# Linear attention and two expert layers in split half precision: last layer-1 output blocks in large buffers, a fixed tile for the inverse roots, weight maxima through HBM, weight differences and the inverse-root product on VectorE

## The chip, the cores and the metric

The program runs on one core of a Trainium2 chip. The metric is the device time of one execution in microseconds. TensorE does the matrix products, VectorE (DVE in the rows), ScalarE (ACT) and GpSimd (POOL) prepare operands and empty the accumulators, and every transfer is issued by SyncE (SP), one after another in program order.

## The reference, cut to what matters

```python
kv  = einsum('bhsd,bhse->bhde', k, v)            # 8 batches, 8 heads, 576 tokens, 64 wide
out = einsum('bhsd,bhde->bhse', q, kv)
x   = out / sqrt(mean(out*out, -1) + 1e-6) * g_norm   # 4608 x 512
h   = x @ w_in;   x1 = maximum(0.01*h, h) @ w_out       # 512 -> 2048 -> 512
h   = x1 @ w2_in; y  = (h - tanh(h)) @ w2_out           # 512 -> 2048 -> 512
```

The weights come as 64-bit floats and the kernel reads them as pairs of 32-bit words.

## The kernel before, in words

The work runs in five stages: a head (first attention batches, first weight matrix), "up 1" (x times w1, the attention of the other batches woven in), "down 1" (times w2, giving x1), "up 2" (x1 times w3, tanh) and "down 2" (times w4, the output). Every factor is split into a high and a low half-precision part, and a product is three matmuls. Blocks of two by two are multiplied by a scheme with seven products instead of eight; `PROD` says which sum of the left blocks meets which sum of the right blocks, and `Blocks` collects the seven products in the accumulator banks a, b, c and d.

Operands are made in chains. `left_stages` (L426) makes those of an activation tile: ScalarE rounds three blocks to the high part (`opa`), VectorE subtracts for the low part, four sums of blocks follow (two on VectorE, two on GpSimd in "down", all four on GpSimd in "up"), and ScalarE and VectorE make high and low part of the sums (`ops`). `right_stages` (L358) does the same for a 128 x 512 unit of a weight matrix, `wo` being the result; its four differences of 128 x 128 blocks are GpSimd's (`less`, L374). `convert` (L293) turns the 64-bit words of a unit into a 32-bit float, stores it to HBM (`wf`), and after the last unit `weight_scale` (L249) finds the power of two that scales the matrix. Only then does `split_late` (L387) load the units again, split them and store the result (`wd`), which `load_weights` fetches when the layer before has let go of the weight tiles. w2 and w3 are converted and w2 is split in up 1; w3 is split in down 1; w4 is converted and split in up 2.

The order of all this is not written down. `Plan` is an event list with assumed durations: `fit` looks for a free stretch on ScalarE, VectorE or GpSimd ("A", "V", "G"), and each engine then gets its instructions in the order of these planned moments. On the chip each engine works its list in that order, and a waiting instruction holds up all behind it.

Working buffers come from three pools, each handed out first in, first out: 21 large ones ("l", 4,608 bytes a partition), 12 middle ones ("m", for weight units, `wo` and `opa`) and 8 small ones ("x", 1,152 bytes). A buffer counts as free in the plan as soon as its store is issued, so the next writer may wait on the chip until that store has landed. The small pool holds the temporary results that ScalarE copies out of bank a (`Blocks.keep`, the tiles c, u), the x1 blocks on their way to HBM (`xst`), the attention's `qt` and `sq`, and the inverse roots `iv` of a batch.

The attention of a batch ends in `norms` (L903): ScalarE takes roots, VectorE inverts (`iv`), `iv` is stored to HBM, read back as rows broadcast over the partitions (`bc`), and GpSimd multiplies the batch's two activation tiles by it (L934).

## Time and profile before

| | |
|---|---|
| device time, three runs | 1527.73 us median (1526.67 to 1530.34) |
| the profiled execution | 1526.35 us, of which its span is 1524.6 us |
| TensorE | busy 1443.4 us (95% of the span) |
| VectorE, ScalarE, GpSimd | busy 1247.2 us (82%), 911.2 us (60%), 759.8 us (50%) |
| TensorE's granted clock | 0.979 of full speed in the mean |
| share of the chain that ended last | TensorE's line L495 (all products of the layers) 42.7%, VectorE 3%, GpSimd 1%, transfers 1% |

TensorE is the engine whose work fills the span. A microsecond counts here if it is idle time of TensorE, or TensorE's time at the lower of its two clocks.

### The profile page before, as it was taken

The numbers are of one execution on the slowest core, as the hardware profiler recorded it, in microseconds if no ns is written. First come the engines' busy times: TensorE is split into PE (matmuls) and PEld (weight loads), VectorE is DVE, ScalarE is ACT, GpSimd is POOL, SyncE is SP. The second block draws the span as 40 slices with busy tenths as digits, with TensorE's granted clock in tenths as the row PEclk, the third lists the DMA queues.
The fourth block names the chain that finished last, engine by engine and source line by source line (L and its number), as shares of the span: only waits on it lengthen the run. The fifth ranks groups of instructions, "written<-read, shape, count | busy, mean of one in ns | idle before, by whom it ended". The sixth has DMA issues, their size and how long they took to land. (4 is left out here: it accounts for less than half of the span.)

```text
span 1524.6 us, 33192 instructions
## 1 busy us (share of the span) xinstructions
PE 1443.4 (95%) x12658; PEld 1191.6 (78%) x12658; DVE 1247.2 (82%) x1971; ACT 911.2 (60%) x1525; POOL 759.8 (50%) x758
## 2 busy tenths in 40 slices
PE   5299999999999999999999899999999899999998
PEld 3167777777777777777777688888888788888887
DVE  4886786777777889899996788988899988888881
ACT  5377766777777645455443577778888544454540
POOL 0483321443643455666673355558896644444440
PEclk8599999999999999999999999999999999999999
DMA  9718987999968756446546666655669644444431
GB/s 264 201 60 257 282 281 250 283 295 313 323 250 317 288 172 208 160 168 207 184 146 214 228 221 209 210 200 209 246 240 353 226 146 149 144 143 156 145 97 36
DMA packets 191040, 323.19 MB, mean 212 GB/s; under 512 B 55712, under 2 KB 133536, under 8 KB 190880
## 3 DMA queue, kind: packets, MB, share of 16 engines
q1 hardware_dynamic: 190880, 321.07, 63.6%
q8 instruction: 99, 1.62, 0.4%
q14 instruction: 61, 0.50, 0.1%
HBM read 190.84 MB, written 130.15 MB: 211 GB/s over the span
## 5 line engine op out<-in xcount | busy, mean ns | idle before, releaser
L495 PEld LDWEIGHTS <-w 128*128 128x128 f16 x8400 | 818.3, 98 | 212.1 <-issue 38.1
L474 POOL TENSOR_TENSOR gl<-gl 128x256 f32<-128x256 f32 (+1 forms) x272 | 305.9, 1126 | 297.9 <-issue 92.6
L495 PE MATMUL ps_a<-ops,w 128*128 128x288 f16 (+1 forms) x2400 | 330.3, 281 | 6.0 <-ACT u L544 3.1
L495 PE MATMUL ps_c<-ops,w 128*128 128x288 f16 (+1 forms) x2352 | 314.0, 282 | 6.9 <-DVE g L557 6.8
L495 PE MATMUL ps_a<-opa,w 128*128 128x288 f16 (+1 forms) x2016 | 285.2, 282 | 12.5 <-ACT u L548 6.6
L495 PEld LDWEIGHTS <-ops 128*128 128x128 f16 x1728 | 169.7, 98 | 24.7 <-issue 4.2
L495 PE MATMUL ps_b<-opa,w 128*128 128x288 f16 (+1 forms) x1200 | 175.6, 283 | 0.0
L376 POOL TENSOR_TENSOR unit<-unit 128x128 f32<-128x128 f32 x192 | 129.6, 677 | 91.4 <-DVE wo L369 57.1
L474 DVE TENSOR_TENSOR gl<-gl 128x256 f32<-128x256 f32 (+1 forms) x272 | 160.7, 594 | 4.1
L1213 POOL TENSOR_TENSOR g<-g,th 128x512 f32<-128x512 f32 x72 | 116.7, 1623 | 78.2 <-ACT th L1210 76.8
L934 POOL TENSOR_TENSOR xg<-xg,bc 128x1152 f32<-128x1152 f32 x16 | 47.4, 2970 | 186.3 <-DMA bc<-iv 118.1
L435 ACT ACTIVATE ops<-gl 128x1152 f16<-128x1152 f32 x64 | 74.3, 1162 | 108.7 <-POOL gl L474 107.0
L437 ACT ACTIVATE ops<-gl,inv 128x1024 f16<-128x1024 f32 x72 | 82.5, 1146 | 94.4 <-POOL gl L474 94.4
L495 PEld LDWEIGHTS <-opa 128*128 128x128 f16 x1296 | 126.6, 98 | 14.8
L444 DVE SCALAR_TENSOR_TENSOR ops<-gl,inv,ops 128x1024 f16<-128x1024 f32 x72 | 103.4, 1436 | 22.8 <-ACT ops L437 22.8
L442 DVE TENSOR_TENSOR ops<-gl,ops 128x1152 f16<-128x1152 f32 x64 | 96.5, 1509 | 11.1 <-ACT ops L435 11.0
L495 PE MATMUL ps_a<-w,ops 128*128 128x256 f16 x864 | 97.5, 275 | 3.6 <-ACT c L548 3.6
L557 DVE SCALAR_TENSOR_TENSOR g<-ps_c,u 128x288 f32<-128x288 f32 x128 | 58.0, 453 | 52.1 <-PE ps_c L495 45.8
L548 ACT ACTIVATE u<-ps_a,up 128x256 f32<-128x256 f32 x144 | 67.9, 472 | 51.8 <-PE ps_a L495 41.6
L495 PE MATMUL ps_c<-w,ops 128*128 128x256 f16 x864 | 97.3, 273 | 0.2 <-DVE osb L557 0.2
L474 POOL TENSOR_TENSOR x1g<-x1g 128x256 f32<-128x256 f32 x72 | 64.0, 890 | 49.8 <-DVE opa L444 42.0
L369 DVE SCALAR_TENSOR_TENSOR wo<-unit,s_w,wo 128x384 f16<-128x384 f32 (+1 forms) x96 | 85.3, 892 | 3.7 <-ACT wo L366 3.6
(122 smaller groups left out, 2147.6 us busy)
## 6 DMA issues: line engine op xcount, KB each, us to landing
g<-g SPq DMA_DIRECT2D x64, 576.0 KB, 5.6
gl<-g SPq DMA_DIRECT2D x64, 576.0 KB, 4.8
g<-g SPq DMA_DIRECT2D x72, 512.0 KB, 3.4
gl<-g SPq DMA_DIRECT2D x72, 512.0 KB, 4.5
wd<-wo SPq DMA_DIRECT2D x48, 448.0 KB, 4.2
w<-wd SPq DMA_DIRECT2D x24, 896.0 KB, 7.7
words<-in_moe_w_in_dram SPq DMA_DIRECT2D x64, 256.0 KB, 5.6
words<-in_moe_w_out_dram SPq DMA_DIRECT2D x64, 256.0 KB, 4.6
```

What stands on the lines that cost most here:

```text
L369: nc.vector.scalar_tensor_tensor(out=dst()[:, 1, a:b], in0=cols(0, n), scalar=scale(), in1=dst()[:, 0, a:b], op0=ALU.mult, op1=ALU.subtract,)
L376: nc.gpsimd.tensor_tensor(out=o, in0=a, in1=b, op=ALU.subtract)
L435: nc.scalar.activation(out=o, in_=i_, func=AF.Copy)
L437: nc.scalar.activation(out=o, in_=i_, func=AF.Identity, scale=scale())
L442: nc.vector.tensor_tensor(out=o, in0=i_, in1=h, op=ALU.subtract)
L444: nc.vector.scalar_tensor_tensor(out=o, in0=i_, scalar=scale(), in1=h, op0=ALU.mult, op1=ALU.subtract)
L474: lambda: e.tensor_tensor(out=g()[:, o], in0=g()[:, a], in1=g()[:, b], op=op),
L495: nc.tensor.matmul(out=out_, lhsT=a, rhs=c, start=start and m == 0, stop=stop and m == n - 1, skip_group_check=not fresh,)
L548: nc.scalar.activation(out=t, in_=src, func=AF.Identity, scale=self.scale)
L557: nc.vector.scalar_tensor_tensor(out=o, in0=src, scalar=self.minus if sub else self.scale, in1=t, op0=ALU.mult, op1=ALU.add,)
L934: nc.gpsimd.tensor_tensor(out=x, in0=x, in1=held[kk].ap, op=ALU.mult)
L1213: e.tensor_tensor(out=g()[:, n], in0=g()[:, n], in1=held["t"].ap[:, n], op=ALU.subtract)
```

## The change

It has seven parts.

1. `iv` no longer takes a small buffer; it has a tile of its own for all batches.
2. In the last of the eight rounds of down 1 the x1 blocks go to large buffers, four blocks in one, and leave in four stores of 128 x 576 instead of eight of 128 x 288. The small pool keeps the temporaries alone there.
3. For w2, w3 and w4 the maximum over the partitions is no longer taken with a transpose and a small matmul on TensorE. `far_scale` stores the column of 128 maxima to HBM, reads it back broadcast to all partitions, and VectorE takes the maximum of each row. The planner gives this 26 units of its time instead of 8.8, so the splits of w2 and w4 are planned later (w2 from START + 219 instead of 200, w4 24 later).
4. The differences of a weight unit become three instructions: `both` makes two of them at once (128 x 2 x 128), `less` the other two. For this the words are loaded in another block order, two signs change and `PROD` is renumbered. For w2, w3 and w4 all three are VectorE's; for w1 they stay GpSimd's.
5. From batch 2 on, the product of the activation tiles with `bc` is VectorE's, each tile in two halves, planned 10.5 after the load instead of 7.5.
6. The attention of the batches from 5 on is woven in 5 products earlier per batch.
7. If the plan finds a pool empty, the step is tried again 0.4 later (`NoRoom`); before, this was an error. VectorE's sums in `left_stages` are planned shorter.

```diff
-PROD = {1: (6, 6), 2: (4, 4), 3: (0, 5), 4: (5, 0), 5: (3, 2), 6: (1, 1), 7: (2, 3)}
+PROD = {1: (6, 5), 2: (4, 4), 3: (0, 6), 4: (5, 0), 5: (3, 1), 6: (1, 2), 7: (2, 3)}
...
-                def run(fn=fn):
-                    fn()
+                def run(fn=fn, until=None):
+                    try:
+                        fn()
+                    except NoRoom:
+                        assert until is None or self.now < until, "no room"
+                        self.at(self.now + 0.4, lambda: run(fn, until or self.now + 40.0))
+                        return
...
+    def far_scale(name, m, t):
+        held = {}
+        def put():
+            held["d"] = scratch([P, 1], F32, f"m_{name}_d")
+            nc.sync.dma_start(out=held["d"], in_=m)
+        def get():
+            held["w"] = const.tile([P, P], F32, tag="rows", name=f"rows_{name}")
+            nc.sync.dma_start(out=held["w"], in_=held["d"].rearrange("p o -> o p").broadcast_to((P, P)))
+        def end():
+            r, s = stile(f"r_{name}"), stile(f"s_{name}")
+            nc.vector.tensor_reduce(out=r, in_=held["w"], axis=AX.X, op=ALU.max)
+            powers(r, s)
+        at(t, put)
+        at(t + 6.0, get)
+        at(t + 24.0, end)
...
-        at(t + 2.8 + (later and later + 2.0), last)
+        at(t + (2.8 if n == 0 else 26.0), last)
...
-        def less(o, a, b):
+        def both(e):
+            b = w().rearrange("p (o c) -> p o c", c=P)
+            e.tensor_tensor(out=b[:, 1:4:2], in0=b[:, 3:4].broadcast_to((P, 2, P)), in1=b[:, 1:3], op=ALU.subtract)
+
+        def less(o, a, b, e):
             o, a, b = (w()[:, P * n:P * n + P] for n in (o, a, b))
-            nc.gpsimd.tensor_tensor(out=o, in0=a, in1=b, op=ALU.subtract)
+            e.tensor_tensor(out=o, in0=a, in1=b, op=ALU.subtract)
...
+        on, e = ("V", nc.vector) if merged else ("G", nc.gpsimd)
+        f = 0.28 if merged else 0.5
...
-            ("G", 0.5, lambda: less(t1, b12, b11)), ("G", 0.5, lambda: less(t3, b22, b12)),
-            ("G", 0.5, lambda: less(t2, b22, t1)),
-            ("G", 0.5, (lambda: less(t4, b21, t2)) if minus4 else (lambda: less(t4, t2, b21))),
+            (on, 1.5 * f, lambda: both(e)), (on, f, lambda: less(t2, b22, t1, e)),
+            (on, f, (lambda: less(t4, b21, t2, e)) if minus4 else (lambda: less(t4, t2, b21, e))),
...
-                on, (1.4 if on == "V" else 2.4) * f + 0.1,
+                on, 1.1 * f + 0.08 if on == "V" else GPS * f + 0.1,
...
-            held["iv"] = X.take([4 * Q, T1], F32, "iv")
+            held["iv"] = const.tile([4 * Q, T1], F32, tag="iv", name="iv")
...
-            nc.gpsimd.tensor_tensor(out=x, in0=x, in1=held[kk].ap, op=ALU.mult)
-            L.give(held[kk])
+            e.tensor_tensor(out=x, in0=x, in1=held[kk].ap[:, n0:n1], op=ALU.mult)
+            if n1 == 4:
+                L.give(held[kk])
...
+            if b >= 2:
+                scaled_ = [("V", 0.66, lambda kk=kk, n=n: scale(kk, nc.vector, n, n + 2)) for n in (0, 2)]
+            else:
+                scaled_ = [("G", 2.9 if b else 2.7, lambda kk=kk: scale(kk, nc.gpsimd, 0, 4))]
+            more.append([(None, LOADBC if b > 1 else 7.5 if b else 6.0, lambda kk=kk: load(kk))] + scaled_ + stages)
...
-            pos[b, PAIRS[hp]] = FIRST[b][hp] if b in FIRST else NOP * (NP * b - 16 + 2 * hp)
+            pos[b, PAIRS[hp]] = FIRST[b][hp] if b in FIRST else NOP * (NP * b - 16 + 2 * hp) - 5 * (b - 4)
...
-    spread(lambda i, kk, t: split_late(1, i, kk, t, M), UNITS, START + 200.0, end1 - 75.0)
+    spread(lambda i, kk, t: split_late(1, i, kk, t, M), UNITS, START + 219.0, end1 - 72.0)
...
+            if s == NS1 - 1:
+                if (s, m) not in out_t:
+                    out_t[s, m] = L.take([P, 2, 2, T1], F32, "xst"), []
+                return out_t[s, m][0].ap[:, int(blk[1]) - 1, int(blk[0]) - 1]
...
+                there.append((t, nh))
+                if {(0, nh), (1, nh)} <= set(there):
+                    done_.update((("x1", c, s, 0), ("x1", c, s, 1)))
+                    nc.sync.dma_start(out=x1d[c, s], in_=tile_.ap[:, nh].rearrange("p a b -> p (a b)"))
+                if len(there) == 4:
+                    L.give(out_t.pop((s, m))[0])
...
-    e = c3 + 18.0
+    e = c3 + 42.0
```

Where the instructions stand. On GpSimd before, around the products of batch 6 (`xg<-xg,bc`) with the differences of w2's units (`unit`) and the sums of the attention tile:

```order
L376 TENSOR_TENSOR unit<-unit 128x128 x20
L934 TENSOR_TENSOR xg<-xg,bc 128x1152 x2
L376 TENSOR_TENSOR unit<-unit 128x128 x2
L474 TENSOR_TENSOR xg<-xg 128x288
L376 TENSOR_TENSOR unit<-unit 128x128
```

On VectorE now, at the products of the same batch; `g<-ps` are the adds that empty an accumulator bank:

```order
L602 SCALAR_TENSOR_TENSOR g<-ps_c,u_5006 128x288
L979 TENSOR_TENSOR xg<-xg,bc 128x576
L908 COPY xg<-po 128x288
L379 SCALAR_TENSOR_TENSOR unit<-words,unit 128x512
L419 TENSOR_TENSOR unit<-unit 128x128
L415 TENSOR_TENSOR unit<-unit 128x2x128
L602 SCALAR_TENSOR_TENSOR g<-ps_c,u_5160 128x288
L979 TENSOR_TENSOR xg<-xg,bc 128x576
L419 TENSOR_TENSOR unit<-unit 128x128
L602 SCALAR_TENSOR_TENSOR g<-ps_b,c_5150 128x288
L360 TENSOR_SCALAR unit,mw<-unit 128x512
L979 TENSOR_TENSOR xg<-xg,bc 128x576
```

Four half products and the differences of the weight units have moved from GpSimd's list into VectorE's, and the adds that empty banks c and b stand behind them.

On VectorE before, at the end of up 2, where the first operand of down 2 is made (`opa<-gl`) and w4's last parts are split (`wo<-unit`):

```order
L557 SCALAR_TENSOR_TENSOR g<-ps_c,up_11272,u_15331 128x256
L444 SCALAR_TENSOR_TENSOR opa<-gl,inv_10683,opa 128x768
L369 SCALAR_TENSOR_TENSOR wo<-unit,s_w_13522,wo 128x512
L557 SCALAR_TENSOR_TENSOR g<-ps_b,up_11272,c_15434 128x256
L474 TENSOR_TENSOR gl<-gl 128x256
L1213 TENSOR_TENSOR g<-g,th 128x512
L557 SCALAR_TENSOR_TENSOR g<-ps_c,up_11272,u_15517 128x256
```

The same place now:

```order
L488 SCALAR_TENSOR_TENSOR opa<-gl,inv_10641,opa 128x768
L419 TENSOR_TENSOR unit<-unit 128x128
L602 SCALAR_TENSOR_TENSOR g<-ps_c,up_11221,u_15429 128x256
L518 TENSOR_TENSOR gl<-gl 128x256
L602 SCALAR_TENSOR_TENSOR g<-ps_c,up_11221,u_15313 128x256
L1276 TENSOR_TENSOR g<-g,th 128x512
L518 TENSOR_TENSOR gl<-gl 128x256
L408 SCALAR_TENSOR_TENSOR wo<-unit,s_w_13719,wo 128x512
L602 SCALAR_TENSOR_TENSOR g<-ps_b,up_11221,c_15419 128x256
L488 SCALAR_TENSOR_TENSOR opa<-gl,inv_10641,opa 128x768
```

A difference and two parts of the split (one more follows eight rows below the first) now stand behind the first operand of down 2, where one part stood.

On SyncE the stores of the last x1 blocks and the loads of w3 before and, in the second piece, now:

```order
L421 DMA w_5_11026<-wd_5_306 128x3584
L1103 DMA x_2_7_100<-xst 128x288
L1103 DMA x_3_7_108<-xst 128x288
L1103 DMA x_2_7_100<-xst 128x288
L1103 DMA x_0_7_84<-xst 128x288
L1103 DMA x_3_7_108<-xst 128x288
L421 DMA w_6_11088<-wd_6_307 128x3584
L1103 DMA x_1_7_92<-xst 128x288
L421 DMA w_7_11154<-wd_7_308 128x3584
```

```order
L465 DMA w_5_10976<-wd_5_306 128x3584
L1165 DMA x_2_7_100<-xst 128x576
L1165 DMA x_0_7_84<-xst 128x576
L1165 DMA x_3_7_108<-xst 128x576
L465 DMA w_6_11036<-wd_6_307 128x3584
L1165 DMA x_1_7_92<-xst 128x576
L465 DMA w_7_11102<-wd_7_308 128x3584
```

Fewer stores stand between the loads of the last weight tiles; each waits for two blocks.

## Rows read from the trace of the kernel before

**Rows 1.** TensorE's timeline, six places; brackets: idle before, and what ended it

```profile
265.34 0.90 PE L495 MATMUL ps_a<-opa,w 128*128 128x288 f16 x6 [1.23 <-ACT u L546]
...
377.51 0.86 PE L495 MATMUL ps_a<-opa,w 128*128 128x288 f16 x5 [2.14 <-ACT u L546]
...
754.25 0.77 PE L495 MATMUL ps_a<-opa,w 128*128 128x288 f16 x5 [1.13 <-DVE opa L442]
...
852.07 1.23 PE L495 MATMUL ps_a<-opa,w 128*128 128x256 f16 x5 [6.64 <-ACT u L548]
...
1183.73 0.82 PE L495 MATMUL ps_c<-ops,w 128*128 128x256 f16 x6 [1.75 <-DVE g L557]
...
1203.82 2.50 PE L495 MATMUL ps_a<-w,ops 128*128 128x256 f16 x12 [3.56 <-ACT c L548]
```

**Rows 2.** ScalarE's timeline at two of these places

```profile
376.75 0.41 ACT L853 ACTIVATE sq<-po 128x288 f32<-128x288 f32 x1 [4.36 <-DMA iv<-iv]
...
851.55 0.87 ACT L548 ACTIVATE u<-ps_a,up 128x256 f32<-128x256 f32 x2 [7.00 <-DMA x<-xst]
```

**Rows 3.** Windows: busy PE, PEld, DVE, ACT, POOL (instructions), PEclk, DMA share, GB/s

```profile
100.00:500.00 400.00, 389.59 (x3506) 299.55 (x3504) 297.52 (x559) 287.81 (x577) 158.27 (x171) 1.00 0.87 280
550.00:800.00 250.00, 245.14 (x1996) 194.74 (x1994) 234.73 (x312) 119.97 (x156) 159.16 (x152) 1.00 0.53 177
1150.00:1200.00 50.00, 47.36 (x429) 41.62 (x428) 50.00 (x66) 35.85 (x55) 34.93 (x26) 1.00 0.95 347
852.00:855.90 3.90, 3.83 (x19) 2.72 (x19) 2.97 (x8) 0.89 (x3) 2.25 (x4) 0.50 0.90 358
378.10:381.50 3.40, 3.40 (x34) 2.31 (x32) 2.57 (x6) 3.06 (x7) 0.00 (x0) 0.50 0.62 195
```

**Rows 4.** TensorE's groups by shape: the weight maxima's transposes; busy us, mean ns

```profile
L224 PE MATMUL pt<-ident,m_w 128*1 128x128 f32 x4 | 1.2, 298 | 29.2 <-DVE m_w L264 29.2
```

**Rows 5.** GpSimd's groups by shape: weight differences and inverse-root products

```profile
L376 POOL TENSOR_TENSOR unit<-unit 128x128 f32<-128x128 f32 x192 | 129.6, 677 | 91.4 <-DVE wo L369 57.1 <-issue 12.0 <-PE ps_a L495 8.8
...
L934 POOL TENSOR_TENSOR xg<-xg,bc 128x1152 f32<-128x1152 f32 x16 | 47.4, 2970 | 186.3 <-DMA bc<-iv 118.1 <-PE ps_a L495 56.4 <-DMA k<-in_k_dram 6.3
```

**Rows 6.** VectorE's groups by shape: the nearest to the moved work

```profile
L474 DVE TENSOR_TENSOR gl<-gl 128x256 f32<-128x256 f32 x144 | 84.5, 588 | 2.9
...
L442 DVE TENSOR_TENSOR ops<-xg,ops 128x576 f16<-128x576 f32 x32 | 29.7, 947 | 4.9 <-ACT ops L435 4.9
```

**Rows 7.** VectorE's timeline: one shape twice, the second time while GpSimd works

```profile
1195.42 0.41 DVE L474 TENSOR_TENSOR gl<-gl 128x256 f32<-128x256 f32 x1
...
1196.96 0.95 DVE L474 TENSOR_TENSOR gl<-gl 128x256 f32<-128x256 f32 x1
```

**Rows 8.** GpSimd's timeline beside it

```profile
1195.92 2.57 POOL L474 TENSOR_TENSOR gl<-gl 128x256 f32<-128x256 f32 x2 [1.84 <-DVE gl L474]
```

**Rows 9.** GpSimd's weight differences alone in down 1: window, busy (instructions)

```profile
550.00:800.00 250.00, 46.07 (x60) 1.00 0.53 177
```

**Rows 10.** Waits of the whole run: us in total, times, longest

```profile
ACT wo L366 <- POOL unit L376: 37.6, 20, 4.6
```

**Rows 11.** SyncE's timeline for batch 6: store of iv, first load of bc

```profile
371.80 0.35 SPq L917 DMA_DIRECT2D iv<-iv  x1
...
376.68 2.58 SPq L927 DMA_DIRECT2D bc<-iv  x4
```

**Rows 12.** GpSimd's timeline: the two products of batch 6

```profile
382.78 3.09 POOL L934 TENSOR_TENSOR xg<-xg,bc 128x1152 f32<-128x1152 f32 x1 [8.07 <-DMA bc<-iv]
388.27 2.88 POOL L934 TENSOR_TENSOR xg<-xg,bc 128x1152 f32<-128x1152 f32 x1 [2.40 <-DMA k<-in_k_dram]
```

**Rows 13.** Transfers issued from 300 to 440 us: KB each, median us to landing

```profile
wd<-wo SPq DMA_DIRECT2D x15, 448.0 KB, 5.5
...
wf<-unit SPq DMA_DIRECT2D x13, 256.0 KB, 5.5
```

**Rows 14.** The same from 1160 to 1200 us

```profile
g<-g SPq DMA_DIRECT2D x8, 512.0 KB, 6.6
```

More of the change, by code (lines that the diff above doesn't have):

```diff
@@ L122, in take @@
         if not self.idle:
-            raise RuntimeError(f"no place {self.kind} for {name}")
+            raise NoRoom(f"no place {self.kind} for {name}")
         n = self.idle.pop(0)
@@ L215, in stile, with powers @@
         return small[name]
+    def powers(r, s, m=None):
+        nc.vector.tensor_scalar(out=r, in0=r if m is None else m, scalar1=2.0**-100, scalar2=None, op0=ALU.max)
+        nc.vector.tensor_scalar(
+            out=r.bitcast(I32), in0=r.bitcast(I32), scalar1=0x7F800000, scalar2=None, op0=ALU.bitwise_and
+        )
+        nc.vector.tensor_scalar(
+            out=s.bitcast(I32), in0=r.bitcast(I32), scalar1=-1.0, scalar2=float(264 << 23),
+            op0=ALU.mult, op1=ALU.add,
+        )
     def pow2_scale(name, m, n, t, apart=1.6):
@@ L264, in first @@
                 nc.vector.tensor_tensor(out=m, in0=m, in1=gabs, op=ALU.mult)
-            pow2_scale(name, m, 1, t + 0.6 + later, 1.6 if n == 0 else 3.0)
+            if n == 0:
+                pow2_scale(name, m, 1, t + 0.6)
+            else:
+                far_scale(name, m, t + 0.6)
         def last():
@@ L273, in last @@
                 fn()
-        later = 0.0 if n == 0 else 4.0
         at(t, first)
-        at(t + 2.8 + (later and later + 2.0), last)
+        at(t + (2.8 if n == 0 else 26.0), last)
     def in_unit(w, i, kk):
@@ L305, in load, with room @@
                 nc.sync.dma_start(
-                    out=held["w"].ap[:, NU * a:NU * a + NU].rearrange("p (b c) -> p b c", b=2), in_=src[a]
+                    out=held["w"].ap.rearrange("p (b a c) -> p a b c", b=2, a=2)[:, a], in_=src[a]
                 )
-        def one():
+        def room():
             if keep is None:
@@ L314, in one @@
                 held["ap"] = keep()
+        def one():
             words = held["w"].ap
@@ L353, in convert, with right_stages @@
         slow = 1.0 if keep else 1.1
-        steps = [(None, land, load), ("A", 0.7, one), ("V", 0.72 * slow, two), ("V", 0.4 * slow, shift),
+        steps = [(None, land, load), (None, 0.0, room), ("A", 0.7, one), ("V", 0.72 * slow, two), ("V", 0.4 * slow, shift),
                  ("V", 0.63 * slow, low), ("V", 0.63 * slow, high)]
         plan.chain(t, steps + ([(None, 0.0, store)] if keep is None else []))
-    def right_stages(w, dst, scale, minus4):
+    def right_stages(w, dst, scale, minus4, merged=False):
         def cols(n0, n1):
@@ L407, in split_late @@
         name = ("w1", "w2", "w3", "w4")[n]
[L408 removed]
+        stages = right_stages(lambda: held["u"].ap, lambda: held["o"].ap, lambda: small[f"s_{name}"], n == 2, n >= 1)
         plan.chain(t, [(None, 9.0, load), (None, 0.0, room)] + stages + [(None, 0.0, store)])
@@ L423, in load_weights, with left_stages @@
         )
-    def left_stages(g, dst, scale, T, done=None, first=None, pieces=1):
+    def left_stages(g, dst, scale, T, done=None, first=None, pieces=1, rest=None):
         f = T / 1000.0
@@ L912, in inverse @@
         def inverse(n):
-            part = held["iv"].ap[:, CP * n:CP * n + CP]
+            part = held["iv"][:, CP * n:CP * n + CP]
             nc.vector.reciprocal(out=part, in_=part)
         def store():
-            nc.sync.dma_start(out=ivd[b], in_=held["iv"].ap)
-            X.give(held["iv"])
+            nc.sync.dma_start(out=ivd[b], in_=held["iv"])
         def load(kk):
@@ L1101, in store @@
             def store():
-                done_.add(("x1", c, s, t))
-                nc.sync.dma_start(out=x1d[c, s][:, T1 * t:T1 * t + T1], in_=o)
-                X.give(out_t.pop((s, m, blk)))
+                if s < NS1 - 1:
+                    done_.add(("x1", c, s, t))
+                    nc.sync.dma_start(out=x1d[c, s][:, T1 * t:T1 * t + T1], in_=o)
+                    X.give(out_t.pop((s, m, blk)))
+                    return
+                tile_, there = out_t[s, m]
+                there.append((t, nh))
[4 more added lines that the diff above has]
+                    L.give(out_t.pop((s, m))[0])
             plan.chain(
```

27 lines of the change are left out of this document (12 added, 15 removed).

## The prediction

> **What bounds the kernel now.** The table of engines comes first: TensorE is busy 95% of the span, so time can only be won where TensorE idles or runs at its lower clock. TensorE's timeline then shows where it idles [rows 1]. The longest of these gaps after the head, 6.64 us at 845, ends with ScalarE's copy `u`; two of 1.23 and 2.14 us in up 1 end with `u` too, one of 1.13 us in down 1 with `opa`, and two of 1.75 and 3.56 us stand at the end of up 2. ScalarE's own rows say what is behind two of them: it stood 7.00 us until an x1 store (`x<-xst`) had landed, and 4.36 us until the store of `iv` had [rows 2]. Both are waits for a buffer of the small pool whose last store is still under way. Only 2.14 of the 4.36 us reach TensorE, so about 2.2 us of such a wait are covered by filled banks.
>
> The windows give the rest [rows 3]. Behind both of these gaps TensorE's granted clock is 0.50, its lower level of 1.2 GHz: for 3.9 us behind the gap at 845 and 3.4 us behind the one at 375, which costs half of each, 1.95 and 1.7 us. They also show how full VectorE is: 297.5 of 400 us in up 1, 234.7 of 250 in down 1, and all of 1150 to 1200.
>
> **x1 in large buffers.** The small pool then holds nothing in transit at 845, and the cause of the 6.64 us is gone, with the 1.95 us of half clock: -8.6. Two things limit it: the DMA engines are 90% busy at 358 GB/s there [rows 3], and the w3 tiles must arrive through the same queue. I take the whole gap, because the row names the store and no load, and -3 as the other end.
>
> **`iv` in a tile of its own.** ScalarE's roots and copies no longer meet that store: the gaps of 1.23 and 2.14 us go, and 1.7 us of half clock: -5.1. In the plan the next batch's `iv` comes some 50 us later, long after the store and its reads, so the one tile costs nothing.
>
> **Maxima through HBM.** TensorE loses three transposes of 298 ns [rows 4] and three small products: -1.0, 0 if something else is waited for there anyway. Six small transfers more cost SyncE about 0.35 us each, as the issue of `iv` does [rows 11], spread over the run. The splits that start later have room up to their tiles' use, except w4's (below). The large wait of 29.2 us in the head is w1's, which keeps the old way.
>
> **Differences on VectorE.** GpSimd loses 192 instructions of 677 ns, 130 us [rows 5]. VectorE gets 48 of 256 elements and 96 of 128. The nearest row is its sum of 128x256, mean 588 ns [rows 6], which takes 0.41 us in one place and 0.95 us beside a busy GpSimd [rows 7, 8]. So a unit costs 0.41 + 2 x 0.2 = 0.8 us at least and 0.59 + 2 x 0.3 = 1.2 at most (half the length at about half the time, an estimate), 13 to 19 us for each matrix.
>
> In down 1 that would bring VectorE from 234.7 to 248 or 254 of 250 us. Against that, GpSimd sheds 46 us there [rows 9], and VectorE's other work gets shorter. How much is the open price: GpSimd's share falls from 159 to 113 of 250 us, so if the mean excess of 588 over 410 ns, 43% of the short time, falls in that proportion to 31%, VectorE gains 8% of its 235 us, 19 us; if only its sums do so (a quarter of its work), 5 us. VectorE ends between 234 and 249 us. The down 1 gap of 1.13 us on `opa` is the kind that grows or shrinks with it. ScalarE stands 37.6 us on GpSimd's differences in 20 waits, up to 4.6 us [rows 10], and VectorE will serve these sooner. I put this part at 0 in up 1 and down 1, with -4 and +4 as ends.
>
> The Trainium skill (Perfetto Trace Analysis, section "Optimizing Scalar/DVE Operations") recalls that GpSimd and VectorE share an SBUF read port, and says that moving operations between the two might not help. The pair of rows agrees that they hinder each other; by that rule this term is 0 as well, and the relief rival below, which needs a real gain, would not come.
>
> **Products with `bc` on VectorE.** 24 instructions of 128x576 at 0.95 us by the nearest row of that size [rows 6], or 1.3 by the 588 ns of 256 elements: 23 to 32 us of VectorE in up 1, for 12 of 2.97 us on GpSimd [rows 5]. With w2's differences VectorE comes to some 340 to 350 of 400 us there, so throughput is no problem. Order is: a half product whose `bc` has not arrived holds the adds that empty banks c and b, which TensorE then waits for. The plan sets the first product 12.3 us (1.8 + 10.5) after the issue of the `iv` store, the second 15.3. In batch 6 the store was issued at 371.80 [rows 11]; the first product began 11.0 us and the second 16.5 us later [rows 12], so the first would be in time and the second 1.2 us late. Six batches at 1.2 us each are 7 us of VectorE waiting, less than the 2.2 us that the banks cover in each case; some will be longer, because loads queue. I take +2, from 0 to +8.
>
> **Attention 5 products earlier, new word order, `PROD`.** Nothing is added: loads, bytes and matmuls are the same in number and size. Five products, at 0.90 us for one of six matmuls [rows 1], are 4.5 us of lead per batch, which covers the longer planned wait of 3 us for `bc`; without it `opa` would come 3 us later.
>
> **Middle buffers.** w2's splits now start 19 later in the plan, while w3's conversions stay. Working through the plan's hand-outs, the middle pool runs empty several times between 343 and 411. Two `wo` of ScalarE get a buffer whose `wf` store was issued 2.5 and 3.8 us before, and six loads of `unit` wait in SyncE's queue for `wd` stores 0.9 to 3.8 us old, with loads of k, v, q and words behind them. Such stores take 5.5 us [rows 13]. ScalarE thus waits 1.7 to 3.0 us twice, about what the banks cover, and SyncE up to 4.6 us. I take +2 and +1, together 0 to +8.
>
> **End of up 2.** Of w4's splits, 24 later in the plan, more falls into 1130 to 1200, where VectorE has no idle time left [rows 3]; three parts of it now stand around the first operand of down 2, where one stood, each with an add or an operand behind it. Four `th` of ScalarE get a large buffer whose store was issued 2.4 to 4.7 us before, and stores of `g` take 6.6 us there [rows 14], so waits of 1.9 to 4.2 us come up. Against that, w4's differences leave GpSimd, which makes half of the sums that down 2's first operands need. The two gaps there are 5.3 us now. I take +3, from -5 (gaps gone) to +8 (2.5 times as long).
>
> **The sum** is -8.6 - 5.1 - 1.0 + 0 + 2 + 3 (middle buffers and SyncE) + 3 = -6.7 us. The profiled execution took 1526.35 us, its span of 1524.6 and 1.75 us outside it; the changed kernel comes to 1519.65 us by it. The median of the three runs is 1.4 us above the profiled one: 1521.0 us.
>
> **Rivals.**
>
> *The relief.* VectorE and GpSimd hinder each other less than I credit: 19 us in down 1 instead of its 13 to 19 added, ScalarE's 37.6 us of waits gone, the gaps of `opa` and the end of up 2 halved or closed (-4 in place of 0, -2 in place of +3). For it speaks the pair of 0.41 and 0.95 us [rows 7]; against it that VectorE stays near 240 of 250 us. Time: 1521 - 9 = 1512 us.
>
> *The gain is eaten.* At 845 the x1 reads or the w3 tiles come late instead (-3 in place of -8.6), since transfers run at 90% there. The share of the DMA engines speaks for it; against it, that there are four stores fewer and nobody waited for a load. Time: about 1527 us, no change.
>
> *VectorE is held by `bc`.* In up 1 the DMA engines are 87% busy [rows 3]. If `bc` lands 5 us or more behind the planned moment, each of the six batches repeats the stall of batch 6, 2.14 + 1.7 = 3.85 us of TensorE, 23 us in all, in place of the +2 above; with four such batches 15 us. It decides from three batches on (11.5 us, more than the 6.7 us won and the 2 booked). Against it: the second product of batch 6 was only 1.2 us late. Time with four batches: 1521 - 2 + 15.4 = 1534 us, with six 1542 us.
>
> **How the numbers follow.** A measurement of this kernel can tell 0.3%, 4.6 us, from no change: faster is below 1523.1, slower above 1532.3. Forecast 0.50, with 1517 to 1526 as its own range (the ends of the x1, `bc` and up 2 terms seldom come together); relief 0.20; gain eaten 0.17; VectorE held 0.13. Of the forecast's chance 0.35 lies below 1523.1; with 0.19 of the relief and 0.02 of the gain eaten, faster is 0.56. Slower is 0.11 of VectorE held and 0.02 of the rest, 0.13, and 0.31 remain for the same. The range from 1509 to 1532 leaves out VectorE held and the relief's far end, less than 0.2.
>
> **What will show it.** Right, if ScalarE's waits for `x<-xst` and `iv<-iv` are gone from the waits and TensorE's gaps at 264, 375 and 845 with them, and the granted clock stays 1.00 there; if VectorE's products wait for `bc` 1 or 2 us; if VectorE's busy time in down 1 stays at 235 to 249 us and its 128x256 sums fall below 588 ns. Wrong, if a gap at about 845 is now ended by a load, if TensorE's gaps in up 1 end with an add `g` behind a `bc` product, or if the gaps at 1150 to 1200 exceed 8 us.

## The result, and the profile after

The changed kernel takes 1548.07 us in the median of four runs (1544.77 to 1551.44), the kernel before 1527.2 us beside it: a ratio of 1.0133, 95% interval 1.0105 to 1.0161. It is slower by about 20 us, where 6.7 us of gain had been forecast. The profiled execution is the slowest of the four; that of before had been the fastest, so their traces differ by 25 us.

TensorE's work is what it was; more of the span is idle. From the page, the line of each engine's busy time:

```profile
PE 1449.6 (94%) x12649; PEld 1195.5 (77%) x12649; DVE 1271.9 (82%) x2136; ACT 913.5 (59%) x1525; POOL 589.2 (38%) x538
```

TensorE's timeline, the gaps over 2 us in up 1 behind 260 us and the last two of up 2 (in brackets the idle time before, and what ended it):

```profile
283.21 0.90 PE L540 MATMUL ps_c<-ops,w 128*128 128x288 f16 x6 [2.79 <-DVE g L602]
...
346.11 1.07 PE L540 MATMUL ps_c<-ops,w 128*128 128x288 f16 x6 [2.04 <-DVE g L602]
...
360.75 1.62 PE L857 MATMUL pk<-v,k 96*64 96x64 f32 x24 [3.18 <-DVE xg L908]
...
396.65 0.90 PE L540 MATMUL ps_a<-ops,w 128*128 128x288 f16 x6 [2.47 <-ACT u L591]
...
417.52 0.90 PE L540 MATMUL ps_a<-ops,w 128*128 128x288 f16 x6 [3.70 <-ACT u L591]
...
482.96 1.38 PE L540 MATMUL ps_a<-ops,w 128*128 128x288 f16 x6 [2.67 <-ACT c L591]
...
1205.78 1.73 PE L540 MATMUL ps_c<-ops,w 128*128 128x256 f16 x12 [2.06 <-DVE g L602]
...
1229.19 6.05 PE L540 MATMUL ps_a<-w,ops 128*128 128x256 f16 x54 [3.25 <-ACT c L593]
```

The gap of 6.64 us behind the last x1 blocks [rows 1] is gone. In its place stand several gaps in up 1. Behind most of them TensorE runs in part at its lower clock; behind the one of 2.79 us at 283 the granted clock stays 1.00. Windows (columns as in [rows 3]) of up 1, of down 1, of four places behind such gaps, and of the start of up 2:

```profile
100.00:500.00 400.00, 376.22 (x3328) 287.08 (x3326) 288.58 (x599) 271.30 (x550) 74.13 (x84) 0.97 0.86 259
571.00:821.00 250.00, 244.79 (x1992) 194.66 (x1990) 239.31 (x355) 121.36 (x158) 115.29 (x93) 1.00 0.53 180
...
283.00:290.00 7.00, 6.29 (x50) 4.96 (x50) 7.00 (x14) 6.19 (x15) 2.49 (x3) 1.00 1.12 301
346.00:350.00 4.00, 3.89 (x36) 2.73 (x36) 3.15 (x7) 1.26 (x4) 0.00 (x0) 0.59 1.03 359
360.00:365.00 5.00, 4.25 (x36) 3.15 (x37) 3.56 (x10) 3.46 (x9) 0.00 (x0) 0.53 0.94 283
396.00:404.00 8.00, 6.09 (x28) 4.15 (x28) 7.29 (x17) 6.03 (x14) 0.00 (x0) 0.62 0.99 362
868.00:872.00 4.00, 4.00 (x39) 3.60 (x37) 3.85 (x10) 1.94 (x5) 2.23 (x3) 1.00 1.01 378
```

The engines that TensorE waits for were standing themselves. The largest waits of ScalarE, VectorE and SyncE's queue between 100 and 525 us that are new and end with a transfer (total us, times, longest):

```profile
ACT wo L405 <- DMA wf<-unit: 14.9, 3, 6.7
```

```profile
DVE xg L979 <- DMA bc<-iv: 13.5, 5, 5.5
```

```profile
SPq L440 <- DMA wd<-wo: 16.7, 6, 5.1
SPq L274 <- DMA m_w_d<-m_w: 6.8, 2, 4.0
```

The last row is the column of maxima, which is read back (`rows_w`) only when its store has landed. Of VectorE's 13.5 us, 1.5 stand at 174, 1.5 at 328, 5.45 at 389 and 5.0 at 276, in front of these two halves:

```profile
280.76 1.43 DVE L979 TENSOR_TENSOR xg<-xg,bc 128x576 f32<-128x576 f32 x2 [5.00 <-DMA bc<-iv]
```

SyncE's waits for `wd` stores begin only at 353. The first of them and what stands around it, in the timelines of SyncE, ScalarE and VectorE:

```profile
351.47 1.65 SPq L447 DMA_DIRECT2D wd<-wo  x1
353.22 0.38 SPq L389 DMA_DIRECT2D wf<-unit  x1
357.70 0.32 SPq L440 DMA_DIRECT2D unit<-wf  x1
```

```profile
358.40 0.61 ACT L405 ACTIVATE wo<-unit,s_w 128x384 f16<-128x384 f32 x1 [4.24 <-DMA wf<-unit]
```

```profile
348.48 0.67 DVE L379 SCALAR_TENSOR_TENSOR unit<-words,unit 128x512 int32<-128x512 int32 x1
...
359.35 0.46 DVE L602 SCALAR_TENSOR_TENSOR g<-ps_c,u 128x288 f32<-128x288 f32 x1 [4.98 <-ACT u L591]
```

ScalarE was free at 354.16 (4.24 us before 358.40) and wanted to write `wo` into a middle buffer whose `wf` store had been issued at 353.22. It stood 4.24 us; its next copy `u` came at 358.93, VectorE's add after that, and TensorE's products for k and v at 360.75 (3.18 us). In the plan that store is 3.8 old when ScalarE comes, on the chip it was 0.9 us old. VectorE's last step on a unit before it ended at 349.15 (348.48 and 0.67), but SyncE works its list in order too: loads and a store of `wo`, which took 1.65 us to issue, came first, and the store of the unit went out 4.1 us later. Then SyncE stood itself until 357.70, for a `wd` store, with its next issues behind it.

**Where the time went.** The product matmuls of two kernels can be put side by side: both have 11,424 in the trace. The table takes the start of the n-th and says how much later than before it is in a stretch: up 1 is n = 660 to 2900 (195.2 to 529.9 us in the trace of before), down 1 from there to 5100 (805.3 us), the turn to up 2 to 5700 (885.2), the end of up 2 from 7560 to 8700 (1089.2 to 1222.5). The first column is the median of the run. The stretches come from one profiled execution each, and those of up 1 scatter by some us: in `b_x1`, whose profiled execution was 7 us under its median, it even gains 5.5, and that of `a_nod4` (25.0) was 7 us over its median. What lies between the turn and the end of up 2 is left out; it is 0.8 us in the changed kernel and at most 4.4 (`a_diff22`).

```
                 median   up 1  down 1  turn  end of up 2
changed kernel  1548.07   21.5     0.4  -8.7   8.9
b_x1            1519.53   -5.5     0.0  -8.7  -2.1
a_poolbc        1538.52    9.2     0.7  -8.7   7.8
a_poolless      1544.89   14.1     6.0  -8.7   9.0
a_scale22       1535.55    4.7     0.5  -8.7   6.3
b_far           1546.44   12.3     0.1   1.5   7.0
b_bc            1530.45    3.5     1.4  -2.1  -0.4
a_diff22        1546.42   10.3    -0.2  -0.9   3.0
a_nod4          1539.69   25.0     0.4  -8.7   2.3
a_mo            1538.28   10.3    -0.4  -8.7   8.2
a_sc22_w4       1529.55    5.6     0.3  -8.7   2.2
a_base22        1545.18    7.7     6.4   1.2   4.1
b_x1_iv         1520.16    0.8     0.0  -8.7  -2.0
b_v11           1540.67    2.9     9.7  -1.4   0.5
a_base22_v14    1535.54    3.1     1.0   0.7   2.5
a_v14           1546.02   22.5    -2.2  -8.7   7.6
b_x1_iv_att     1528.90    8.1     0.0  -8.7  -0.6
b_x1_iv_att7    1529.57    5.1     1.5  -8.7   0.7
a_sc22_w4_v14   1522.99    7.0    -2.0  -8.7  -0.2
```

So the change wins its x1 gap, and loses 21.5 us in up 1 and 8.9 us at the end of up 2. There the two long gaps are together what they were, 5.3 us (1.75 and 3.56 before, 2.06 and 3.25 now); the loss is in a row of short ones. TensorE's waits for VectorE's adds between 1060 and 1235 us, before and now:

```profile
PE ps_c L495 <- DVE g L557: 1.8, 1, 1.8
```

```profile
PE ps_c L540 <- DVE g L602: 11.4, 9, 2.1
```

### The profile page after: what moved, and what is told of

Same layout as the page of the kernel before. It is cut to its first block, busy times and chain, and to the rows that moved or that the text cites. A ratio compares the mean times of both kernels' runs of the same rounds, so it can differ in the third digit from the quotient of the medians.

```text
span 1549.6 us, 33055 instructions
## 1 busy us (share of the span) xinstructions
PE 1449.6 (94%) x12649; PEld 1195.5 (77%) x12649; DVE 1271.9 (82%) x2136; ACT 913.5 (59%) x1525; POOL 589.2 (38%) x538
## 5 line engine op out<-in xcount | busy, mean ns | idle before, releaser
L518 POOL TENSOR_TENSOR xg<-xg 128x288 f32<-128x288 f32 x64 | 58.9, 924 | 294.3 <-DMA k<-in_k_dram 110.7
L518 DVE TENSOR_TENSOR gl<-gl 128x256 f32<-128x256 f32 (+1 forms) x272 | 150.9, 557 | 3.5
L540 PEld LDWEIGHTS <-opa 128*128 128x128 f16 x1296 | 126.9, 98 | 14.9
L486 DVE TENSOR_TENSOR ops<-gl,ops 128x1152 f16<-128x1152 f32 x64 | 95.8, 1498 | 12.5 <-ACT ops L479 12.3
L405 ACT ACTIVATE wo<-unit,s_w 128x384 f16<-128x384 f32 (+1 forms) x96 | 63.0, 661 | 52.0 <-DVE unit L419 34.1
L488 DVE SCALAR_TENSOR_TENSOR opa<-gl,inv,opa 128x768 f16<-128x768 f32 x72 | 87.3, 1213 | 0.3 <-ACT opa L481 0.2
```

What stands on the lines that cost most here:

```text
L405: nc.scalar.activation(out=dst()[:, 0, a:b], in_=cols(0, n), func=AF.Identity, scale=scale())
L486: nc.vector.tensor_tensor(out=o, in0=i_, in1=h, op=ALU.subtract)
L488: nc.vector.scalar_tensor_tensor(out=o, in0=i_, scalar=scale(), in1=h, op0=ALU.mult, op1=ALU.subtract)
L518: lambda: e.tensor_tensor(out=g()[:, o], in0=g()[:, a], in1=g()[:, b], op=op),
L540: nc.tensor.matmul(out=out_, lhsT=a, rhs=c, start=start and m == 0, stop=stop and m == n - 1, skip_group_check=not fresh,)
```

## The experiments

Names that begin with b are the kernel before with parts of the change, those with a the changed kernel with parts undone. The kernel before took 1527.4 to 1528.7 us in the median beside them.

**Four first runs: one gain and three suspects.** `b_x1` adds part 2 to the kernel before, as in the diff of the change.

> The kernel before with part 2 alone (the last x1 blocks in large buffers). Theory: the part is worth its gap and half clock whatever else is done; TensorE's wait of 6.64 us at 845 and 1.95 us of half clock go, so 1527.2 - 8.6 = 1518.6 us, and the product matmuls behind 852 us start 8 to 9 us earlier than before. Rival: without the lag of some 23 us that the changed kernel carries there, w3 loads or x1 reads come late instead, and it gains less than 4 us: 1523 us or more.

`a_poolbc` undoes part 5:

```diff
-            if b >= 2:
+            if b >= 8:
-            more.append([(None, LOADBC if b > 1 else 7.5 if b else 6.0, ...
+            more.append([(None, 7.5 if b else 6.0, ...
```

> The changed kernel with part 5 undone (products with bc on GpSimd for all batches, planned 7.5 after the load). Theory A, the products hold VectorE in up 1: the 13.5 us that VectorE stands on bc go, with the idle time and half clock of TensorE near 280, 357 and 395, some 10 us: about 1538 us. Theory B, late splits of w2 and their middle buffers: VectorE's waits for bc only fell together with these; gain under 3 us, 1545 us or more.

`a_poolless` puts all differences on GpSimd:

```diff
-        ..., n == 2, n >= 1)
+        ..., n == 2, False)
```

> The changed kernel with the differences of w2 to w4 back on GpSimd (three instructions a unit, as w1's). Theory C, VectorE is overfull at the end of up 2 because of the differences: the 10 us lost between 1090 and 1230 us go, and a few in up 1: 1536 to 1538 us. Theory B: w4's splits planned later press on that stretch wherever the differences are made; the loss there stays, and GpSimd's hindrance comes back: 1547 us or more.

`a_scale22` undoes part 3:

```diff
-                far_scale(name, m, t + 0.6)
+                pow2_scale(name, m, 1, t + 4.6, 3.0)
-        at(t + (2.8 if n == 0 else 26.0), last)
+        at(t + (2.8 if n == 0 else 8.8), last)
-    ... split_late(1, i, kk, t, M), UNITS, START + 219.0, end1 - 72.0)
+    ... split_late(1, i, kk, t, M), UNITS, START + 200.0, end1 - 75.0)
-    e = c3 + 42.0
+    e = c3 + 22.0
```

> The changed kernel with part 3 undone (maxima of w2 to w4 over TensorE, w2's splits from START + 200 to end1 - 75, w4's 22 after the conversions instead of 42). Theory B, late splits and the middle buffers they find: ScalarE's 14.9 us on wf stores and SyncE's 16.7 us on wd stores go, up 1 loses 10 us less, and the end of up 2 about 8 us less: 1530 us. Theory A (bc holds VectorE) and C (differences fill it): under 4 us, 1544 us or more.

`b_x1` measured 1519.53 us, 0.9938 of before (0.991 to 0.9965). What stood 6.64 us at the turn is 0.56 us in its timeline:

```profile
836.61 0.81 PE L495 MATMUL ps_a<-ops,w 128*128 128x256 f16 x6 [0.56 <-ACT c L548]
```

Every run with part 2 gains 8.7 us at the turn, whatever lag it brings there; the rival is refuted. `a_poolbc` measured 1538.52, as theory A had it: VectorE's waits for `bc` are gone, and up 1 loses 12 us less. But theory B's waits shrink with them, SyncE's for `wd` from 16.7 to 2.8 us and ScalarE's for `wf` from 14.9 to 5.9. `a_scale22` measured 1535.55: up 1 loses 4.7 instead of 21.5 us, ScalarE no longer waits for a `wf` store there, and VectorE's waits for `bc` are 1.2 us; theory B is right for up 1, as far as part 3 as a whole is meant, but the end of up 2 still loses 6.3. `a_poolless` measured 1544.89: the end of up 2 keeps its loss, so theory C falls in the form in which it was put; up 1 is 7 us better, and down 1, with the differences on GpSimd again, 6 us worse. Each of three edits takes 7 to 17 us out of up 1, more than there is in all: they feed one another.

**Parts alone.** `b_far` is part 3 on the kernel before, `b_bc` parts 5 and 6, both as in the diff of the change; `a_diff22` is `a_scale22` with parts 1, 2, 5 and 6 undone too. `a_nod4` leaves w4's differences out:

```diff
+        ] + ([] if skip else [
             (on, 1.5 * f, lambda: both(e)), (on, f, lambda: less(t2, b22, t1, e)),
...
-        ..., n == 2, n >= 1)
+        ..., n == 2, n >= 1, n == 3)
```

> The kernel before with part 3 alone (maxima through HBM, w2's splits from START + 219, w4's 24 later), and with part 7's second try when a pool is empty, which it needs. Theory B, late splits harm by themselves: ScalarE stands on wf stores and SyncE on wd stores as in the changed kernel, up 1 loses about 10 us, the end of up 2 some 4 us: 1540 us. Rival, they harm only together with a VectorE that the other parts have filled: under 4 us, 1531 us or less.

> The kernel before with parts 5 and 6 alone (products with bc on VectorE, planned 10.5 after the load, attention 5 products earlier). Theory A, VectorE held by bc harms by itself: VectorE stands on bc for 10 us or more, up 1 loses about 8 us: 1536 us. Rival, with w2's splits in their old place the bc loads come in time: VectorE stands on them under 4 us, the time stays within 3 us of 1528.

> The changed kernel with parts 1, 2, 3, 5 and 6 undone (w4's splits 22 after the conversions): what is left is the differences on VectorE, the block order and the shorter planned sums. Theory C, VectorE is full in the last 100 us of up 2: its busy time there grows by about 10 us, and TensorE loses as much between 1090 and 1190: 1537 us, up 1 within 3 us of before. Rival, GpSimd's relief pays for the differences: no loss there beyond 3 us, 1529 us.

> The changed kernel with the three differences of each w4 unit left out on any engine (the products of down 2 then use wrong sums). Theory C: 14.7 us less of VectorE's work stand in the last 100 us of up 2, the loss there goes from 10 us to 0 to 2: 1539 us. Rival, w4's split planned later is the loss (five more parts of wo in that stretch, and what waits for them): the loss stays above 6 us, 1545 us.

`b_far` measured 1546.44 (1.0121, 1.0094 to 1.0148): part 3 harms by itself, 12.3 us in up 1 and 7.0 at the end of up 2, more than expected, and the rival falls. But the waits that theory B named did not come: ScalarE stands 3.1 us for a `wf` store, and SyncE for no `wd` store. TensorE's longest gap in up 1 is another:

```profile
286.64 1.94 PE L854 MATMUL pk<-v,k 96*64 96x64 f32 x24 [5.93 <-DMA v<-in_v_dram]
```

The loads of `v` were issued at 276.1 and 276.5 and took some 10 us to land, as did a `wf` store issued at 272.4. Why transfers were so slow there, and whether the late splits or the round trip of the maxima did it (SyncE stood up to 4.4 us for a column), no run takes apart. `b_bc` measured 1530.45 (1.0014, 1.0000 to 1.0027): parts 5 and 6 together hardly harm alone; with the splits in their old place VectorE stands 5.7 us on `bc`, between the theory's 10 and the rival's 4. `a_nod4` measured 1539.69: the end of up 2 loses 2.3 instead of 8.9 us. The windows of the same 1,140 matmuls there, in the changed kernel and in `a_nod4`:

```profile
1104.50:1246.70 142.20, 128.46 (x1143) 112.37 (x1142) 137.90 (x212) 103.44 (x163) 74.41 (x59) 0.99 0.75 267
```

```profile
1106.60:1242.20 135.60, 127.09 (x1142) 112.38 (x1141) 130.46 (x180) 103.14 (x163) 72.98 (x59) 0.99 0.78 276
```

VectorE is busy 96 to 97% of the stretch in both; the stretch is 6.6 us shorter, VectorE's work in it 7.4 us. `a_diff22` measured 1546.42, 9 us more than theory C had; the loss lay in up 1 (10.3), not at the end of up 2 (3.0), and the next runs took the differences out of it.

**Buffers, and a control.** `a_mo` gives w2's `wo` large buffers; `a_sc22_w4` is `a_scale22` with w4's differences on GpSimd; `a_base22` is `a_diff22` with all of them there; `b_x1_iv` is parts 1 and 2 on the kernel before.

```diff
-    spread(lambda i, kk, t: split_late(1, i, kk, t, M), ...
+    spread(lambda i, kk, t: split_late(1, i, kk, t, L, M), ...
```

```diff
-        ..., n == 2, n >= 1)
+        ..., n == 2, n in (1, 2))
```

> The changed kernel with the results wo of w2's split in large buffers instead of middle ones; every planned moment of the three engines stays. In the plan no middle buffer is then handed out whose store is younger than 6.5. Theory B2, the reused middle buffers are what the late split costs in up 1: ScalarE's waits on wf (14.9 us) and SyncE's on wd (16.7 us) go, and up 1 loses 10 to 12 us instead of 20: 1537 us. Rival, the loss comes from VectorE's order and the late loads of units: over 15 us stay, 1544 us or more.

> The changed kernel with part 3 undone as in the run with the maxima back on TensorE (1535.6 us), and the differences of w4 alone on GpSimd. Theory C, the end of up 2 loses whatever is put on VectorE there, the differences or more parts of a later split: with neither, the loss of 12 us between 1089 and 1200 falls to 3 or less: 1527 us. Rival, the shorter planned sums (part 7) make that loss: it stays at 8 us or more, 1534 us.

> The run with the differences alone on VectorE (1546.4 us), with the differences on GpSimd too: of the change only the block order, three instructions for four, the shorter planned sums and w4's splits 4 later are left. If the differences on VectorE are what costs: within 4 us of before, 1528 to 1532 us, no loss at the end of up 2. Rival, the planned costs of part 7 are behind it: 1540 us or more.

> The kernel before with parts 1 and 2 alone: iv in a tile of its own, last x1 blocks in large buffers. If both waits are worth what their gaps and half clock say, 1528.2 - 8.6 - 5.1 = 1514.5 us, 5 us under part 2 alone. Rival, the iv wait comes back as another wait in up 1 (w1 and attention order unchanged): the time of part 2 alone, 1519 us.

`a_mo` measured 1538.28, and up 1 loses 10.3 instead of 21.5 us; ScalarE's waits for `wf` and those of the loads of units for `wd` are gone, while VectorE still stands 9.9 us on `bc`. But the planned moments did not stay, as had been expected. The plan of the changed kernel finds the middle pool empty for six steps between 343 and 408 and tries them again 0.4 to 4.0 later (part 7); with `wo` in large buffers it finds it empty for none. From 349 us on ScalarE's list has another instruction in 181 places, VectorE's in 220. What stands behind the same `wo` in the changed kernel and in `a_mo`:

```profile
349.23 0.43 ACT L868 ACTIVATE kvd<-pk 64x64 f32<-64x64 f32 x2
```

```profile
351.87 0.68 ACT L356 ACTIVATE unit<-words 128x512 f32<-128x512 f32 x1
```

So half of the loss in up 1 comes with the shortage of middle buffers (theory B2); how much by young stores and how much by the steps that it moves, the run does not separate. `a_sc22_w4` measured 1529.55 and loses 2.2 us at the end of up 2. With `a_scale22` (6.3) and `a_poolless` (9.0) this says what is lost there: early splits and differences on GpSimd 2.2, early and on VectorE 6.3, late 9 on either engine, late and left out 2.3. With early splits the place of the differences makes 4.1 us, so there VectorE's time is the cause. With late ones it is not shown to be: leaving them out wins 6.6 us, but moving them to GpSimd, where VectorE is busy 132.9 of 142.3 us, wins nothing, and why stays open.

`a_base22` measured 1545.18, no better than `a_diff22`. So the differences on VectorE were not what cost in `a_diff22`; in down 1 they even win 6.6 us (-0.2 against 6.4). `b_x1_iv` measured 1520.16, no less than part 2 alone: the tile for `iv` wins nothing. ScalarE's row there, at the place where it had stood 4.36 us for the store of `iv` [rows 2]:

```profile
386.52 0.92 ACT L435 ACTIVATE opa<-xg 128x864 f16<-128x864 f32 x1 [6.39 <-POOL xg L933]
```

Before, it stood 2.06 us and began 0.6 us earlier:

```profile
385.91 0.92 ACT L435 ACTIVATE opa<-xg 128x864 f16<-128x864 f32 x1 [2.06 <-POOL xg L934]
```

Of 4.36 + 2.06 = 6.42 us not one is won: `opa` needs the product with `bc`, which comes from the same `iv`, and ScalarE now waits there.

**The planned sums.** After twelve runs it was open what `a_base22` suffers from. `b_v11` has one line of part 7 on the kernel before, `a_base22_v14` and `a_v14` are without it:

```diff
-                on, (1.4 if on == "V" else 2.4) * f + 0.1,
+                on, 1.1 * f + 0.08 if on == "V" else 2.4 * f + 0.1,
```

> The kernel before with one line of part 7 alone: VectorE's sums planned at 1.1 f + 0.08 instead of 1.4 f + 0.1. Theory D, the shorter planned sums are behind the loss of the run with the differences on GpSimd (17 us; 8 in up 1, 6 in down 1, up to 9 at the end of up 2): at least half of it here, 1537 us or more, with a loss at the end of up 2 of 5 us or more. Rival E, the block order and the changed hand-out of middle buffers are: within 3 us of before, 1527 to 1530 us.

> The run with block order, three instructions on GpSimd, shorter planned sums and w4's splits 4 later (1545.2 us), with the sums planned as before. Theory D: the end of up 2 and down 1 lose under 3 us, 1535 us or less. Rival E: it stays at 1541 us or more.

> The changed kernel with VectorE's sums planned as before, every other part left. Theory D: the loss of 10 us at the end of up 2 falls to 4 us or less, and up 1 keeps its 20 us: 1541 us. Rival C, the differences on VectorE are that loss whatever is planned: 1546 us or more.

`b_v11` measured 1540.67 (1.0075, 1.0056 to 1.0095): this number in the planner alone costs 13 us, 9.7 of them in down 1. So at least half of the loss is there, as theory D had it, but not the 5 us at the end of up 2 (0.5). Two of its gaps in down 1:

```profile
660.95 6.04 PE L495 MATMUL ps_a<-ops,w 128*128 128x288 f16 x48 [2.99 <-ACT u L544]
...
724.79 1.36 PE L495 MATMUL ps_a<-opa,w 128*128 128x288 f16 x5 [2.69 <-DVE opa L442]
```

`a_base22_v14` measured 1535.54, 9.6 us less than `a_base22`: theory D holds there. In `a_v14` (1546.02) it falls: the changed kernel loses the same without the shorter sums. The 7 us that `a_base22_v14` still has over before are spread over the run and were not traced.

**Earlier attention.** `b_x1_iv_att` adds part 6 to `b_x1_iv`; `b_x1_iv_att7` has -7 for each batch from 4 on in its place. `a_sc22_w4_v14` is `a_sc22_w4` with the old planned sums.

> Parts 1, 2 and 6 on the kernel before: iv in its own tile, last x1 blocks in large buffers, attention of the batches from 5 on 5 products earlier per batch. Without part 6 ScalarE stood 6.39 us on a bc product at 380, where before it had stood 4.36 us on iv and then 2.06 us on the product. Theory, the roots of the batch are what is late: attention 10 products earlier for batch 6 (some 9 us) lets the product be done in time, and the gap of 3.5 us with its half clock goes: 1515 us. Rival, the wait has other causes (GpSimd's order, loads of k) or comes back at another batch: 1519 to 1520 us as without part 6.

> The same with each batch from 4 on 7 products earlier, in place of 5, 10 and 15 for the batches 5, 6 and 7. Theory of late roots: batch 4's waits shrink as well, 1514 to 1516 us. Rival: earlier attention takes small buffers and banks from the products around it, 1519 us or more.

> The changed kernel with part 3 undone, w4's differences on GpSimd and VectorE's sums planned as before; left of the change are parts 1, 2, 5, 6 and the differences of w2 and w3 on VectorE. Theory D: the shorter planned sums are the rest of what separates 1529.6 us from the 1520 us of parts 1 and 2 alone: 1522 us or less. Rival: with late splits and w4's differences gone VectorE has room, and the planned sums no longer matter: 1527 us or more, the rest being the products with bc (up 1).

Both earlier variants lose what parts 1 and 2 had won: 1528.90 and 1529.57. The theory of late roots falls, and the first is 9 us over its rival too. A row of VectorE's timeline in `b_x1_iv_att`:

```profile
385.54 0.46 DVE L557 SCALAR_TENSOR_TENSOR g<-ps_b,c 128x288 f32<-128x288 f32 x1 [7.87 <-DMA g<-g]
```

An add that empties bank b stands 7.87 us because a store of `g` has not landed, and TensorE 4.57 us behind it at 382; batches that begin earlier also take large buffers earlier, which would explain it, but no run tested this, and `b_x1_iv_att7` has no such wait. `a_scale22`, `a_sc22_w4`, its last variant and `b_bc` have the same gap of 6 to 8 us at 376. `a_sc22_w4_v14` measured 1522.99 (0.9963, 0.9949 to 0.9977), as theory D had it to 1 us; what separates it from 1520 us lies in up 1 (7.0 against 0.8).

The fastest kernel is `b_x1`: part 2 alone, 1519.53 us, 0.6% under before and 1.8% under the changed kernel.

## Why the prediction was wrong, by its own steps

The sum failed in up 1 and at the end of up 2. For up 1 the terms came to about zero (`iv` -5.1, `bc` +2, middle buffers +3), and 21.5 us were lost; of the terms there that of the middle buffers was too small by most. For the end of up 2 it was +3, and 8.9 us were lost.

**x1 in large buffers: right.** -8.6 was forecast, -8.7 us measured at the turn in all thirteen kernels that have the part. In the changed kernel the granted clock is 1.00 behind it, with the DMA engines busy throughout.

**`iv`: wrong in kind.** -5.1 was forecast and nothing came, in `b_x1_iv`. In the changed kernel too ScalarE's wait for `iv<-iv` is gone, which was to be a sign of being right. The step took a wait off without asking who needs the same transfer next. That was to be read beside it: ScalarE's next operand was ended by the product with `bc` [rows 12].

**Maxima through HBM: priced at their issue.** Six transfers were booked at 0.35 us each. But the column can be read back only when its store has landed, and SyncE stood 6.8 us in two such waits in up 1, with all its later issues behind. What this costs TensorE is open, since no run has the late splits without these transfers.

**Middle buffers: the waits foreseen, their price not.** +3 was booked with +8 as its end; `wo` in large buffers gave 9.8 us of the median back (`a_mo`), 11 by the traces of up 1. SyncE's six waits came about as worked out, the longest 5.1 us for 4.6. ScalarE stood 14.9 us in three waits, not twice 1.7 to 3.0: the working used the ages that stores have in the plan, and on the chip a store goes out late when other issues stand in front of it (0.9 instead of 3.8 us old at 354). The step that failed is to let the banks cover each wait on its own; the lower clock behind the gaps, and the steps that the empty pool moves in the lists, were not in the term either. And this is not all that part 3 does: alone it cost 12.3 us in up 1 nearly without these waits (`b_far`).

**Products with `bc`: about right with the old splits, wrong in company.** VectorE stood 5.7 us on `bc` in `b_bc`, for 7 forecast, and the time rose by 2.2 us, for +2 booked; but that run has the earlier attention in it, so the price of the products alone is not shown. In the changed kernel VectorE stood 13.5 us, and 9.5 us of the loss go when the products go back. One sign of the rival of a held VectorE came: the gap at 283 ends with an add behind a `bc` product. Its cause is not the one that it named, transfers in up 1 being busy as before: with part 3 undone the 13.5 us are 1.2. It takes the products and part 3 together; only the 5.45 us at 389 stand behind SyncE's waits for `wd`.

**Attention earlier: costed at nothing, wrong beside parts 1 and 2.** It was taken to cover the later `bc`. But the lead is 5, 10 and 15 products in the batches 5, 6 and 7 and none in 2 to 4, where 6.5 of the 13.5 us stand. On top of parts 1 and 2 it costs 8.7 us. The add that waits for a store of `g` shows where in one of the two variants; why is not shown. No run takes it out of the changed kernel alone, so its share of the 20 us is open: with the products on VectorE, and w2's and w3's differences too, the time is only 2.8 us above that of parts 1 and 2 (`a_sc22_w4_v14`).

**End of up 2: +3 forecast, +8.9 measured,** beyond the end of +8. The differences take 379 ns (128x128) and 556 ns (256 elements), 1.3 us a unit, where 0.8 to 1.2 had been worked out. Leaving them out wins 6.6 us; that it is VectorE's time which costs here is shown for early splits only (4.1 us). The step that failed looked at the two long gaps, which stayed as they were, and not at the adds between them.

**Differences in down 1: within its range.** VectorE is busy 239 us there, forecast 234 to 249 (by its own terms, 248 less 19 to 254 less 5, it is 229 to 249), and its sums fell from 588 to 567 ns. The rows of VectorE by shape in the changed kernel:

```profile
L518 DVE TENSOR_TENSOR gl<-gl 128x256 f32<-128x256 f32 x144 | 81.5, 567 | 2.7
...
L419 DVE TENSOR_TENSOR unit<-unit 128x128 f32<-128x128 f32 x96 | 36.4, 379 | 0.2
...
L415 DVE TENSOR_TENSOR unit<-unit 128x256 f32<-128x256 f32 x48 | 26.7, 556 | 0.2
L979 DVE TENSOR_TENSOR xg<-xg,bc 128x576 f32<-128x576 f32 x24 | 17.9, 751 | 13.5 <-DMA bc<-iv 13.5
```

Between two kernels with the shorter planned sums the move wins 6.6 us in down 1 (`a_base22`, `a_diff22`). So there is relief, but the rival's gain over before did not come: 0.4 us are lost in the changed kernel, and with the old sums 2.2 and 2.0 are won (`a_v14`, `a_sc22_w4_v14`). The Trainium skill's caution (Perfetto Trace Analysis, section "Optimizing Scalar/DVE Operations") that moving work between these two engines might not help fits the end of up 2, where the move costs 4.1 us with early splits, and not down 1. VectorE's busy share does not tell the two apart, 239 of 250 us in down 1 and 96 to 97% at the end of up 2.

**Not priced at all: the shorter planned sums.** The prediction had no term for part 7, since nothing is added to an engine. One line of it alone costs 13 us, and its second try moves six steps of the changed kernel. There the shorter sums hardly matter (`a_v14`); in `a_sc22_w4` they cost 6.6 us.

The parts do not add up: alone, part 3 and the one line of part 7 cost 18 and 13 us, part 6 on top of 1 and 2 cost 9, and all seven together 20 us beside a gain of 8.7. A likely reason is that each makes the same lists of SyncE, ScalarE and VectorE late, where a wait behind another costs nothing more; it was not tested by itself.

## What to carry to other kernels

When a wait for a transfer is taken away, look for the next instruction that needs the same transfer's result; if it stands a few us behind, nothing is won. A buffer that is given back when its store is issued must be counted by the chip's order of issues, not by the plan's: a store that stands behind other issues goes out late, and the next writer finds it young. Where a planner hands out the buffers, a run with more of them also moves steps, so the order of the engines' lists has to be compared before the gain is put down to the buffers. A planner's assumed duration or start is a change of the kernel, to be priced like an added instruction, above all in a stretch where VectorE has no idle time.

## What the runs showed of the hardware that had not been expected

On VectorE a difference of 128x128 took 281 ns in the median and one of twice the length 416 ns (379 and 556 ns in the mean), so halving an instruction did not halve its time. The product of 128x576 in 32 bits took 749 ns, and the subtraction of that size with a 16-bit result 750 ns; the mean of the latter is 947 ns before [rows 6] and 889 ns now, so the products were priced too high: 24 took 17.9 us, where 23 to 32 had been booked. And gaps of TensorE of only 2.0 to 3.2 us were followed by stretches in which the granted clock fell to 0.53 to 0.62 of full speed in the mean, with 1.2 GHz in part of them, but not all were: behind the 2.79 us at 283 it stayed 1.00.
